# Pooled attention and a mixture of adapters on one core: queries of chunks 4 to 7 turned by DMA, the second batch's sums spread, and the gates' path one period later

## The chip, the cores and the metric

The kernel runs on one core of a Trainium2 chip. Its five engines work in order, each on its own queue of instructions: TensorE (PE, products of matrices and transposes), VectorE (DVE), ScalarE (ACT, here the exponentials), GpSimd (POOL) and SyncE (SP, which issues the transfers). They wait for one another by semaphores. The metric is the time of one execution on the device in microseconds (us); a smaller time is better. The median of three runs before the change is 381.48 us.

## What is computed

```python
def _attn_ref(q, kv, w_sr):                # q (4, 12288, 128), kv (4, 384, 32, 128)
    kv_pool = kv.reshape(B, H // 4, 4, W // 4, 4, C).mean(axis=(2, 4))
    k = v = kv_pool.reshape(B, -1, C) @ w_sr          # 768 keys for each batch
    s = q @ k.transpose(0, 2, 1) / np.sqrt(C)
    a = np.exp(s - s.max(-1, keepdims=True))
    a /= a.sum(-1, keepdims=True) + 1e-09
    return a @ v

def _moe_ref(x, w_gate, A, B):             # x: the 49152 rows of the attention
    logits = x @ w_gate                    # 8 adapters, the best two of each row
    ...
    w = softmax of the two chosen logits
    delta = sum over the two chosen e of w[e] * ((x @ A[e]) @ B[e])    # rank 16
    return x + delta
```

The weights `w_sr`, `w_gate`, `A` and `B` are small; `q`, `kv` and the result are 25 MB each in fp32.

## The kernel before

**Tiles and periods.** The 49152 queries are 96 chunks of 512 (`NCH`), 24 for each of the four batches (`CPB`). The loop of L653 takes c from 2 to 94, and I call one turn of it period c. In period c PE makes three groups of scores for chunks ahead (`scores(x, r)`, r = 0 to 2, each two products L303 for 256 of the 768 keys, followed by an exponential of 128x1024 on ACT, L304), weighs the values of chunk c - 1 in two halves (`weigh`, L315, twelve products each), and does the adapters' work of earlier chunks. `next_scores` takes the next group from the list `todo`. The scores go through two PSUM buffers, `stile`, which the keys' and values' steps use as well, so a group waits until the exponential two groups before has read its buffer.

**After the weighing.** `normalise(c - 1)` on DVE divides by the sum and finds the maxima of the logits (L322, L326, L333); it frees the one PSUM buffer of `weigh`. In even periods `gate(c // 2 - 1)` makes the arguments of a pair's gates on POOL (L342 to L346), and behind it `cast_q` turns the queries of a later pair of chunks into f16 (L107). In odd periods `gate_tanhs((c - 3) // 2)` takes the tanh on ACT (L358), and at the period's end `send_gates` turns the gates on DVE (L402) and stores them in a DRAM tile (L403). `load_gates` fetches them back, spread over the partitions (L410). `gated_hidden(x)` multiplies the hidden values by them on DVE (L420); `up` and `give` make the output rows (L463, L477) and store a pair of chunks (L495). How many periods after its weighing a chunk's hidden values are made is `lag`: 9 for chunks under 57, then 8, 7 and 6. At lag 9 a pair's fetch is issued three periods after its store's, at the start of an even period.

**The queries.** `load_q` reads 1024 queries, `cast_q` makes them f16, `turn_q` transposes them by a DMA (L114) into `qT`; there are two buffers of `q32`, three of `q16`, five of `qT`. The queries of chunks 0 to 7 go another way: `q0` and `q1`, 1 MB each, are transposed in fp32 on PE (`queries`, L567) and copied out by ACT (chunks 0 to 3) or DVE (4 to 7).

**The keys and values.** `load_row` reads a quarter of a kv tile (512 KB); `sum_row` and `sum_cols` add it up, for batch 0 on DVE, for the others on POOL (L173, L177, L178). The steps `pooled_transposed`, `values` and `keys` follow on PE and ACT. `plan(b)` writes down in which period each load (`at`), each add (`sm`) and each step (`st`, then two and three periods later) stands. `squares` and `ranges` gather sums for a check of the values' size.

**What sets the order.** It is written out by hand: each engine does its instructions in program order. SyncE issues nearly all transfers from one queue, in the order: in an odd period query load, output store, kv rows, gates' store; in an even one gates' fetch, turn, kv rows. A wait in it holds up all that follow.

**The start.** Ahead of the loop the three tiles of batch 0 are added up as they land (L593 to L596), `tile_keys` and `tile_values` make keys and values, and the first scores are put between them; `warm` gives PE empty products to do. Before period 2 the groups of chunks 0 and 1 and the groups (2,0), (2,1), (3,0) have been made. At the ends of periods 6 and 8 a fourth group is made (L717).

Of the kernel before, what the change touches and what calls it, by code (L numbers as in the profile page):

```python
# [10 lines left out]
FP32 = mybir.dt.float32  # L11
# [4 lines left out]
AF = mybir.ActivationFunctionType  # L16
# [5 lines left out]
def kernel(  # L22
# [10 lines left out]
    nc = tc.nc  # L33
    P = 128
    B, N, C = q.tensor.shape
# [5 lines left out]
    NTOK = 512  # L41
    NS = NTOK // P
    VW = C + E + 1
    CPB = N // NTOK
    NCH = B * CPB
# [8 lines left out]
    qpool = ctx.enter_context(tc.tile_pool(name="qpool", bufs=3))  # L54
# [17 lines left out]
    mm = nc.tensor.matmul  # L72
# [8 lines left out]
    NT = NJ // 2  # L81
# [16 lines left out]


    def load_q(i):  # L100
        q32[i] = qpool.tile([P, 2, NS * C], FP32, tag="q32", name="q32", bufs=2)
        nc.sync.dma_start(q32[i], qflat[i * HROWS:(i + 1) * HROWS].rearrange(
            "(k p s) c -> p k (s c)", p=P, s=NS))

    def cast_q(i):
        q16[i] = qpool.tile([P, HROWS], F16, tag="q16", name="q16", bufs=3)
        nc.gpsimd.tensor_copy(q16[i], q32[i].rearrange("p k n -> p (k n)"))  # L107

    def new_qT(i):
        qT[i] = qpool.tile([P, 2 * NS, P], F16, tag="qT", name="qT", bufs=5)  # L110
# [1 line left out]
    def turn_q(i):  # L112
        new_qT(i)
        nc.sync.dma_start(qT[i], q16[i], transpose=True)  # L114
# [3 lines left out]
    for t in range(NT):  # L118
        load_kv(0, t)
        if t == 0:  # L120

            nc.sync.dma_start(q0, qflat[0:GROWS].rearrange("(k p s) c -> p k s c", p=P, s=NS))
    nc.sync.dma_start(q1, qflat[GROWS:2 * GROWS].rearrange("(k p s) c -> p k s c", p=P, s=NS))

    w_in = const.tile([P, P], FP32)
    nc.scalar.dma_start(w_in, w_sr)
# [53 lines left out]
    def stile(name):  # L180
        return ps_s.tile([P, 2, NTOK], FP32, tag="sg", name=name)
# [27 lines left out]
    def tile_keys(t, between=lambda: None):  # L209

        k = slice(2 * t * P, 2 * (t + 1) * P)
        kp_ps = ps_t.tile([P, 2 * P], FP32, tag="tp", name="kp_ps")
        for u in range(2):
            mm(kp_ps[:, u * P:(u + 1) * P], kvt[0, t][:, 0, u, 0:C], id_f32, is_transpose=True,
               start=(u == 0), stop=(u == 1), skip_group_check=True)
        if t < NT - 1:
            nc.scalar.activation(kpT[0][:, k], kp_ps, AF.Copy)
        else:
            nc.vector.tensor_copy(kpT[0][:, k], kp_ps)
        between()  # L220
        k_ps = mtile([P, 2 * P], name="k_ps")
        mm(k_ps, w_sr_sb, kpT[0][:, k], start=True, stop=True)
        nc.scalar.activation(kfT[0][:, k], k_ps, AF.Copy)

    def tile_values(t):
        v_ps = mtile([P, 2, C + E], name="v_ps")
# [28 lines left out]
    def plan(b):  # L255
        c0 = CPB * (b - 1)
        if b == 1:
            at = [2, 2, 3, 4, 5, 6, 6, 8, 9, 10, 10, 12]
            sm = [5, 5, 7, 9, 9, 11, 13, 13, 15]
            st = [10, 14, 18]  # L260
        else:
            at = [-11, -9, -7, -5, -5, -3, -1, 1, 1, 3, 5, 7]
            sm = [-3, -1, 1, 3, 5, 7, 9, 11, 13]
            st = [4, 10, 16]
        for i, k in enumerate(at):
            loads.setdefault(c0 + k, []).append((b, i // 4, i % 4))
# [291 lines left out]

    for i in range(4):
        new_qT(i)

    def queries(g, k, t):

        for i in range(NS):
            mm(t[:, i * P:(i + 1) * P], (q0, q1)[g][:, k, i], id_f32, is_transpose=True,  # L567
               start=(i == 0), stop=(i == NS - 1), skip_group_check=True)
        qt = qT[2 * g + k // 2][:, k % 2 * NS:(k % 2 + 1) * NS].rearrange("p s t -> p (s t)")
        if g == 0:  # L570
            nc.scalar.activation(qt, t, AF.Copy)
        else:
            nc.vector.tensor_copy(qt, t)
# [13 lines left out]
    a_bf = const.tile([P, P], BF16)  # L587
    b_half = const.tile([P, P], FP32)
    b_bf = const.tile([P, P], BF16)
    load_q(4)  # L590
    load_q(5)
    cast_q(4)
    for t in range(NT):  # L593
        for d in range(1, 4):
            sum_row(0, t, d, nc.vector)
        sum_cols(0, t, nc.vector)  # L596
        if t == 0:
            nc.vector.tensor_copy(a_bf.rearrange("p (r e) -> p e r", e=E),
                                  a_f.rearrange("p (e r) -> p e r", e=E))
# [3 lines left out]
    tile_keys(0, lambda: queries(0, 0, x_bank()))  # L603
    queries(0, 1, x_bank())
    scores(0, 0)
    tile_values(0)
    queries(0, 2, x_bank())
    scores(1, 0)
    queries(0, 3, x_bank())
    scores(2, 0)  # L610
    scores(3, 0)
    warm(8)
    tile_keys(1)
    warm(2)
    scores(0, 1)
    tile_values(1)
    scores(1, 1)
    weigh(0, 0)
    warm(2)
    tile_keys(2, lambda: queries(1, 0, stile("q_ps")[:, 0]))  # L620
    queries(1, 1, t_bank())
    scores(0, 2)
    tile_values(2)
    scores(2, 1)
    queries(1, 2, t_bank())
    weigh(0, 1)
    scores(1, 2)
    normalise(0)

    todo = [(x, r) for x in range(2, NCH) for r in range(3) if (x, r) not in ((2, 0), (2, 1), (3, 0))]

    def next_scores():
        if todo:
            scores(*todo.pop(0))

    NQ = NCH // GRP

    def lag(c):

        return next(v for m, v in LAGS if c < m)
# [3 lines left out]
    for x in range(OWN):  # L647
        made.setdefault(x + lag(x), []).append(x)
        ups.setdefault(x + lag(x - 3) + 1, []).append(x)
    for p in range(OWN // 2):  # L650
        sent[2 * p + 3] = p
        fetched[2 * p + 3 + {9: 3, 8: 2, 7: 2, 6: 1}[lag(2 * p + 1)]] = p
    for c in range(2, NCH - 1):  # L653
        b, k = divmod(c, CPB)
        if c in fetched and lag(2 * fetched[c] + 1) > 8:
            load_gates(fetched[c])
        if c % 2 == 0 and c // 2 + 3 < 2 * NQ:
            turn_q(c // 2 + 3)
        if c % 2 and (c + 11) // 2 < 2 * NQ:
            load_q((c + 11) // 2)  # L660
        if c == 2:
            load_q(6)
        next_scores()
        if c == 2:
            queries(1, 3, t_bank())
        weigh(c - 1, 0)
        if c == NCH - 2:
            down(c - 4, stile("h_ps")[:, 0])
            apply_gate(c - 4)
        next_scores()  # L670
        if c >= 3 and c % 2 == 1:
            gate_tanhs((c - 3) // 2)
        for x in made.get(c, ())[:-1]:
            gated_hidden(x, t_bank())
        for x in ups.get(c, ()):
            up(x, None if x == ups[c][-1] else t_bank())
            give(x)
        if c in fetched and lag(2 * fetched[c] + 1) <= 8:
            load_gates(fetched[c])
        weigh(c - 1, 1)  # L680
        prep_step(c)
        if c == CUT + 5:
# [36 lines left out]

# [285 lines left out]
```

## Time and profile before

| | us |
|---|---|
| median of three runs | 381.48 |
| lowest, highest | 381.07, 382.75 |
| the profiled execution, whole | 382.61 |
| its span, first to last instruction | 380.8 |
| PE busy | 362.9 |
| ACT busy | 311.1 |
| DVE busy | 301.7 |
| POOL busy | 224.4 |

A row of an order in time gives the start, the time, engine, line, operation, the tiles (out<-in) with their shapes, and how many were merged; in brackets stand the idle time before it and who ended it. "L303" is a line of the kernel. PEld is PE's loading of weights. The windows give the busy time of each engine in a stretch, and the share in which the DMA engines were busy; a share over 1 means that transfers were waiting on one another. A chain of waits is followed back from the last instruction; a row of it gives start, length and what the time went to.

### The profile page before, as it was taken

To read this page: it belongs to the slowest core of one execution; us is meant where nothing else is said; L and a number is where in the kernel's file an instruction comes from. 1 tells how busy PE (TensorE), PEld (TensorE's weight loads), DVE (VectorE), ACT (ScalarE), POOL (GpSimd) and SP (SyncE) were. 2 spreads that over 40 slices of the span, in tenths; PEclk is the share of its full clock that TensorE was granted. 3 is DMA by queue.
4 is the path that set the end of the run, shared out by engine and by line. 5 is a ranking of instruction groups with operands and counts; after the bars stand their busy time and mean duration, and the time that the engine had idled before them with its cause. 6 is when DMAs were issued, how large, how long until landed. Compare 5 with 4: busy or idle time off the path is not lost.

```text
span 380.8 us, 10632 instructions
## 1 busy us (share of the span) xinstructions
PE 362.9 (95%) x3962; PEld 267.7 (70%) x3963; DVE 301.7 (79%) x951; ACT 311.1 (82%) x392; POOL 224.4 (59%) x374
## 2 busy tenths in 40 slices
PE   4989989999999999999999999999999999999993
PEld 1447757677777777777777777777777777767682
DVE  2686556878788888888888888888888898898983
ACT  1547999888888888888888988988888888888853
POOL 1002699996898877764689877755524335232244
PEclk9999999999999999999999999999999999999998
DMA  8996799999999999999999999999899799883325
GB/s 253 364 386 205 203 271 303 300 310 256 365 296 302 309 326 259 312 288 320 320 289 304 338 279 299 278 246 243 175 298 256 196 226 243 182 220 119 136 86 195
DMA packets 93465, 100.47 MB, mean 264 GB/s; under 512 B 56676, under 2 KB 56932, under 8 KB 93412
## 3 DMA queue, kind: packets, MB, share of 16 engines
q1 hardware_dynamic: 91940, 99.58, 96.1%
q8 instruction: 31, 0.51, 0.6%
q10 hardware_dynamic: 1472, 0.20, 0.3%
q14 instruction: 22, 0.18, 0.1%
HBM read 62.33 MB, written 25.90 MB: 232 GB/s over the span
## 4 chain that ended last, share of the span: by engine, by line
PE 73%; DMA 9%; DVE 7%; POOL 7%; issue 2%; ACT 1%; SPq 0%; ACTq 0%; POOLq 0%; DVEq 0%
PE xps L315 30%; PE sg L303 26%; PE d_ps L463 5%; PE t_ps L382 4%; DMA kvt<-in_kv_dram 4%; PE h_ps L417 4%; DMA b_f<-in_moe_B_dram 3%; POOL kvt L173 2%; DVE xn L326 2%; DMA ge<-g_h 2%; DVE ht L420 1%; PE v_ps L197 1%; DVE top L333 1%; POOL q L107 1%; POOL kvt L177 1%
## 5 line engine op out<-in xcount | busy, mean ns | idle before, releaser
L304 ACT ACTIVATE tt<-sg 128x1024 f16<-128x1024 f32 x288 | 277.5, 1022 | 34.8 <-PE sg L303 33.9
L303 PE MATMUL sg<-qT,kfT 128*128 128x512 f16 x576 | 170.1, 379 | 2.4 <-ACT tt L304 1.6
L315 PEld LDWEIGHTS <-tt 128*128 128x128 f16 x2304 | 148.0, 98 | 27.0 <-DVE xn L326 17.2
L315 PE MATMUL xps<-vext,tt 128*128 128x137 f16 x2256 | 166.3, 223 | 0.0
L477 DVE TENSOR_TENSOR osb<-d_ps,xn 128x512 f32<-128x512 f32 x85 | 58.7, 691 | 30.6 <-PE d_ps L463 30.4
L342 POOL TENSOR_TENSOR arg<-xn,top 128x64 f32<-128x64 f32 x47 | 14.8, 315 | 107.3 <-DVE top L333 91.5
L326 DVE TENSOR_TENSOR xn<-xps,rinv_all 128x548 f32<-128x548 f32 x94 | 68.5, 728 | 3.2
L303 PEld LDWEIGHTS <-kfT 128*128 128x128 f16 x576 | 49.3, 98 | 27.1 <-issue 3.9
L173 POOL TENSOR_TENSOR kvt<-kvt 128x1024 f32<-128x1024 f32 x27 | 63.8, 2362 | 0.2
L107 POOL CAST q<-q 128x1024 f16<-128x1024 f32 x44 | 45.7, 1038 | 26.6 <-DMA q<-in_q_dram 26.6
L420 DVE SCALAR_TENSOR_TENSOR ht<-ge,h_ps 128x512 bf16<-128x512 f16 x87 | 58.5, 672 | 0.6 <-DMA ge<-g_h 0.3
L463 PEld LDWEIGHTS <-ht 128*128 128x128 bf16 x368 | 27.2, 97 | 23.6 <-DVE ht L420 3.9
L333 DVE MAX8 top<-xn 128x8 f32<-128x8 f32 x376 | 35.1, 156 | 6.3
L393 DVE COPY xt<-t_ps 128x512 bf16<-128x512 bf16 x92 | 36.7, 399 | 0.0
L382 PE MATMUL t_ps<-id_bf,xn 128*128 128x128 bf16 x376 | 36.3, 219 | 0.0
L463 PE MATMUL d_ps<-b_bf,ht 128*128 128x128 bf16 x340 | 32.9, 219 | 0.3 <-DVE ht L420 0.2
L417 PE MATMUL h_ps<-xt,a_bf 128*128 128x512 bf16 x86 | 32.6, 379 | 0.1
L322 DVE RECIPROCAL rinv_all<-xps 128x4 f32<-128x4 f32 x94 | 17.1, 182 | 15.4 <-PE xps L315 13.1
L382 PEld LDWEIGHTS <-xn 128*128 128x128 bf16 x376 | 26.0, 98 | 0.3
L345 POOL TENSOR_SCALAR msk<-msk 128x64 f32<-128x64 f32 x47 | 20.2, 429 | 4.1
L346 POOL TENSOR_TENSOR arg<-arg,msk 128x64 f32<-128x64 f32 x47 | 15.1, 321 | 3.9
L344 POOL TENSOR_TENSOR arg<-arg,msk 128x64 f32<-128x64 f32 x47 | 15.0, 320 | 3.7
(149 smaller groups left out, 229.4 us busy)
## 6 DMA issues: line engine op xcount, KB each, us to landing
kvt<-in_kv_dram SPq DMA_DIRECT2D x48, 512.0 KB
q<-in_q_dram SPq DMA_DIRECT2D x44, 512.0 KB
out_dram<-osb SPq DMA_DIRECT2D x44, 512.0 KB
ge<-g_h SPq DMA_DIRECT2D x45, 256.0 KB
q<-in_q_dram SPq DMA_DIRECT2D x2, 1024.0 KB
out_dram<-osb SPq DMA_DIRECT2D x8, 256.0 KB
g_h<-g_sb SPq DMA_DIRECT2D x45, 16.0 KB
qT<-q SPq DMA_TRANSPOSE x44
```

The costliest lines, as they stand in the source:

```text
L107: nc.gpsimd.tensor_copy(q16[i], q32[i].rearrange("p k n -> p (k n)"))
L173: eng.tensor_tensor(v[:, 0], v[:, 0], v[:, d], op=ALU.add)
L303: mm(sg[:, k], kfT[b][:, j * P:(j + 1) * P], qc, start=True, stop=True)
L304: nc.scalar.activation(tt[c][:, 2 * r:2 * r + 2], sg, AF.Exp, bias=0.0, scale=scale)
L315: mm(o, tt[c][:, j, s * P:(s + 1) * P], vext[b][:, j, 0:VW], start=(j == 0 and s % 2 == 0), stop=(j == NJ - 1 and s % 2 == 1), skip_group_ ...
L326: nc.vector.tensor_tensor(xn[c].rearrange("p (b s) v -> p b s v", b=2), xv, ri.rearrange("p (b s) -> p b s", b=2).unsqueeze(3).broadcast_t ...
L333: nc.vector.max(gin[c // 2][:, (c % 2) * NS + s], xn[c][:, s, C:C + E])
L382: mm(columns(t_ps, c, s), src[:, s], id_bf, is_transpose=True, start=(s == 0), stop=(s == NS - 1), skip_group_check=True)
L417: mm(h_ps, a_bf, xT[c], start=True, stop=True)
L420: nc.vector.scalar_tensor_tensor(hgT[c].rearrange("p (k a) t -> p k (a t)", k=2), gE[c // 2][:, h:h + NS // 2].rearrange("p a t k -> p k ( ...
L463: mm(dps[c][:, s], columns(hgT[c], c, s), b_bf, start=(s == 0 and fresh), stop=(s == NS - 1), skip_group_check=True)
L477: nc.vector.tensor_tensor(osb[:, lo:hi], d, xn[c][:, lo:hi, 0:C], op=ALU.add)
```

## The change

It has these parts:

- The queries of chunks 4 and 5 and of 6 and 7 (`q32[2]`, `q32[3]`) are loaded in halves into the place of `q1`, with the loads of the next two pairs between; they are cast (`cast_half` on DVE for the first, `cast_q(3)` on POOL for the second) and turned by DMA ahead of the loop. The products of `queries` for them, and their copies on DVE, go. `q32` has three buffers.
- In the start, groups (3,1) and (2,2) are made ahead of the loop, (2,1) earlier than before; the extra groups at the ends of periods 6 and 8 go. The third tile's keys are copied by DVE. Four warming products go.
- For the second batch (`b == 1`) loads, adds and steps stand in other periods.
- At lag 9 the tanh, the turning and the store of a pair's gates stand one period later, in even periods, and so does the fetch, now at the start of odd periods, ahead of the query load.
- The squares of the first two batches stand two periods later.

```diff
     def load_q(i):
-        q32[i] = qpool.tile([P, 2, NS * C], FP32, tag="q32", name="q32", bufs=2)
+        q32[i] = qpool.tile([P, 2, NS * C], FP32, tag="q32", name="q32", bufs=3)
...
-    nc.sync.dma_start(q1, qflat[GROWS:2 * GROWS].rearrange("(k p s) c -> p k s c", p=P, s=NS))
+
+    def load_half(i):
+        q32[i] = q1[:, 2 * i - 4:2 * i - 2].rearrange("p k s c -> p k (s c)")
+        nc.sync.dma_start(q32[i], qflat[i * HROWS:(i + 1) * HROWS].rearrange(
+            "(k p s) c -> p k (s c)", p=P, s=NS))
+
+    load_half(2)
+    load_q(4)
+    load_half(3)
+    load_q(5)
...
-        nc.scalar.activation(kfT[0][:, k], k_ps, AF.Copy)
+        if t < NT - 1:
+            nc.scalar.activation(kfT[0][:, k], k_ps, AF.Copy)
+        else:
+            nc.vector.tensor_copy(kfT[0][:, k], k_ps)
...
         if b == 1:
-            at = [2, 2, 3, 4, 5, 6, 6, 8, 9, 10, 10, 12]
-            sm = [5, 5, 7, 9, 9, 11, 13, 13, 15]
-            st = [10, 14, 18]
+            at = [2, 2, 3, 4, 5, 5, 6, 8, 9, 9, 11, 13]
+            sm = [3, 5, 6, 8, 9, 10, 12, 14, 16]
+            st = [9, 13, 19]
...
-    load_q(4)
-    load_q(5)
+    new_q16(2)
+    cast_q(3)
     cast_q(4)
+
+    def cast_half(k):
+        nc.vector.tensor_copy(q16[2][:, k * NTOK:(k + 1) * NTOK], q32[2][:, k])
...
-    warm(8)
+    warm(6)
     tile_keys(1)
     warm(2)
     scores(0, 1)
     tile_values(1)
     scores(1, 1)
     weigh(0, 0)
-    warm(2)
-    tile_keys(2, lambda: queries(1, 0, stile("q_ps")[:, 0]))
-    queries(1, 1, t_bank())
+
+    def during():
+        cast_half(0)
+        scores(2, 1)
+
+    tile_keys(2, during)
+    cast_half(1)
+    turn_q(2)
+    turn_q(3)
+    scores(3, 1)
     scores(0, 2)
     tile_values(2)
-    scores(2, 1)
-    queries(1, 2, t_bank())
+    scores(1, 2)
     weigh(0, 1)
-    scores(1, 2)
+    next_scores()
     normalise(0)
...
+    tanhs = {}
+    for p in range(NCH // 2 - 2):
+        tanhs[2 * p + 3 + (lag(2 * p + 1) > 8)] = p
     for p in range(OWN // 2):
-        sent[2 * p + 3] = p
-        fetched[2 * p + 3 + {9: 3, 8: 2, 7: 2, 6: 1}[lag(2 * p + 1)]] = p
+        sent[2 * p + 3 + (lag(2 * p + 1) > 8)] = p
+        fetched[2 * p + 3 + {9: 3 + (lag(2 * p + 3) > 8), 8: 2, 7: 2, 6: 1}[lag(2 * p + 1)]] = p
...
-        if c == 2:
-            queries(1, 3, t_bank())
...
-        if c >= 3 and c % 2 == 1:
-            gate_tanhs((c - 3) // 2)
+        if c in tanhs:
+            gate_tanhs(tanhs[c])
...
-        if k in (17, 19, 21) and b + 1 < B:
+        k0 = 19 if b == 0 else 17
+        if k in (k0, k0 + 2, k0 + 4) and b + 1 < B:
             if b == 0:
-                squares(0, (k - 17) // 2)
-            squares(b + 1, (k - 17) // 2)
+                squares(0, (k - k0) // 2)
+            squares(b + 1, (k - k0) // 2)
...
-        if c in (6, 8):
-            next_scores()
```

More of the change, by code (lines that the diff above doesn't have):

```diff
@@ L105, in cast_q, with new_q16 @@
     def cast_q(i):
+        new_q16(i)
+        nc.gpsimd.tensor_copy(q16[i], q32[i].rearrange("p k n -> p (k n)"))
+    def new_q16(i):
         q16[i] = qpool.tile([P, HROWS], F16, tag="q16", name="q16", bufs=3)
-        nc.gpsimd.tensor_copy(q16[i], q32[i].rearrange("p k n -> p (k n)"))
     def new_qT(i):
@@ L557, in all_ok, with queries @@
         nc.vector.tensor_scalar(bad, last, tot, full, op0=ALU.add, op1=ALU.not_equal)
-    for i in range(4):
+    for i in range(2):
         new_qT(i)
-    def queries(g, k, t):
+    def queries(k, t):
         for i in range(NS):
-            mm(t[:, i * P:(i + 1) * P], (q0, q1)[g][:, k, i], id_f32, is_transpose=True,
+            mm(t[:, i * P:(i + 1) * P], q0[:, k, i], id_f32, is_transpose=True,
                start=(i == 0), stop=(i == NS - 1), skip_group_check=True)
[L569 to L573, printed above, removed]
+        qt = qT[k // 2][:, k % 2 * NS:(k % 2 + 1) * NS].rearrange("p s t -> p (s t)")
+        nc.scalar.activation(qt, t, AF.Copy)
     def x_bank():
@@ L602, with next_scores @@
     warm(18)
-    tile_keys(0, lambda: queries(0, 0, x_bank()))
-    queries(0, 1, x_bank())
+    todo = [(x, r) for x in range(2, NCH) for r in range(3) if (x, r) not in ((2, 0), (2, 1), (3, 0), (3, 1))]
+    def next_scores():
+        if todo:
+            scores(*todo.pop(0))
+    tile_keys(0, lambda: queries(0, x_bank()))
+    queries(1, x_bank())
     scores(0, 0)
     tile_values(0)
-    queries(0, 2, x_bank())
+    queries(2, x_bank())
     scores(1, 0)
-    queries(0, 3, x_bank())
+    queries(3, x_bank())
     scores(2, 0)
     scores(3, 0)
-    warm(8)
+    warm(6)
     tile_keys(1)
```

4 lines of the change are left out of this document (removed).

## The prediction

> **What bounds the kernel now.** I read the page first, then the busy time by stretches, then TensorE's instructions in order of time, then what the other engines wait for, and last SyncE's queue.
>
> ```profile
> span 380.8 us, 10632 instructions
> PE 362.9 (95%) x3962; PEld 267.7 (70%) x3963; DVE 301.7 (79%) x951; ACT 311.1 (82%) x392; POOL 224.4 (59%) x374
> 31.00:95.00 64.00, 61.93 (x682) 45.71 (x681) 42.92 (x154) 57.46 (x72) 49.59 (x67) 1.00 1.04 272
> 95.00:260.00 165.00, 165.00 (x1872) 124.97 (x1869) 139.45 (x448) 145.99 (x183) 125.78 (x186) 1.00 1.13 301
> ```
>
> In the last two rows the columns are the stretch, its length, busy time of PE, PEld, DVE, ACT and POOL, the granted clock, the DMA engines' share and GB/s. From 95 to 260 us PE is busy without a gap: what the change does off PE there can only cost. Between 31 and 95 us PE lacks 2 us outright, and its order shows more. The first group of twelve weighted sums (L315) of a period marks it; I call its start the period's start.
>
> ```profile
> 36.26 0.89 PE L315 MATMUL xps<-vext,tt 128*128 128x137 f16 x12
> ...
> 45.51 0.89 PE L315 MATMUL xps<-vext,tt 128*128 128x137 f16 x12
> ...
> 49.32 0.59 PE L303 MATMUL sg<-qT,kfT 128*128 128x512 f16 x2 [0.66 <-ACT tt L304]
> 49.75 0.88 PE L315 MATMUL xps<-vext,tt 128*128 128x137 f16 x12
> ...
> 56.80 0.59 PE L303 MATMUL sg<-qT,kfT 128*128 128x512 f16 x2 [0.72 <-ACT tt L304]
> 57.23 0.88 PE L315 MATMUL xps<-vext,tt 128*128 128x137 f16 x12
> ...
> 60.41 0.88 PE L315 MATMUL xps<-vext,tt 128*128 128x137 f16 x12
> ```
>
> Periods 3, 4 and 5 take 45.51 - 36.26 = 9.25 us, 3.08 each. The next four, 6 to 9, take 14.90 us, where four of 3.08 make 12.33: 2.57 us more. Two of them hold a fourth score group (the extra ones after periods 6 and 8), and PE waits there for the exponentials on ACT. Some 0.10 of it is period 9's first hidden product, so the extra groups cost 2.5 us.
>
> ```profile
> 67.42 0.88 PE L315 MATMUL xps<-vext,tt 128*128 128x137 f16 x12
> ...
> 75.68 0.88 PE L315 MATMUL xps<-vext,tt 128*128 128x137 f16 x12
> ...
> 82.69 0.88 PE L315 MATMUL xps<-vext,tt 128*128 128x137 f16 x12
> ...
> 90.60 0.88 PE L315 MATMUL xps<-vext,tt 128*128 128x137 f16 x12
> ...
> 97.61 0.88 PE L315 MATMUL xps<-vext,tt 128*128 128x137 f16 x12
> ...
> 105.09 0.88 PE L315 MATMUL xps<-vext,tt 128*128 128x137 f16 x12
> ```
>
> ```profile
> 67.29 0.32 ACT L358 ACTIVATE gw_all<-arg 128x64 f16<-128x64 f32 x1 [0.83 <-DVE xn L326]
> ```
>
> ```profile
> 66.94 0.32 POOL L346 TENSOR_TENSOR arg<-arg,msk 128x64 f32<-128x64 f32 x1
> ```
>
> The first six rows are the three pairs of periods (12-13, 16-17, 20-21) in which a tile's values and keys are made: 8.26, 7.91 and 7.48 us for the same work. The third is free of stalls; the first two lose 0.78 + 0.43 = 1.2 us. The two rows after them, of ACT and of POOL, show why: the tanh (L358) starts at 67.29, right after POOL's last gate step ends at 67.26, with 0.83 us of ACT lost before it. The exponentials stand behind it. (The row names DVE, which had long been done.)
>
> **The change, part by part.**
>
> *Scores moved forward.* Two groups, (2,2) and (3,1), move from periods 6 and 8 ahead of the loop, where ACT has room. The loop's periods 6 to 9 become plain: **-2.5**.
>
> *Queries 4 to 7 by DMA.* Sixteen fp32 transposes and three of their four DVE copies leave the stretch before 33 us, the fourth the start of period 2; two DVE casts, one POOL cast and two DMA transposes enter.
>
> ```profile
> 26.79 0.42 DVE L178 TENSOR_TENSOR kvt<-kvt 128x256 f32<-128x256 f32 x1
> ...
> 27.74 0.42 DVE L219 COPY kp_keep<-kp_ps 128x256 f32<-128x256 f32 x1 [0.53 <-PE kp_ps L214]
> ...
> 28.22 0.70 PE L222 MATMUL k_ps<-kp_keep,w_sr_sb 128*128 128x256 f32 x2
> ...
> 30.04 1.94 ACT L304 ACTIVATE tt<-sg 128x1024 f16<-128x1024 f32 x2 [0.70 <-PE sg L303]
> 30.04 1.36 SPq L114 DMA_TRANSPOSE qT<-q  x1
> ...
> 31.17 0.88 PE L315 MATMUL xps<-vext,tt 128*128 128x137 f16 x12
> ```
>
> ```profile
> 31.00:32.00 1.00, 1.00 (x17) 0.97 (x15) 0.63 (x1) 0.97 (x2) 0.00 (x0) 1.00 0.68 136
> 32.00:33.00 1.00, 1.00 (x8) 0.58 (x6) 0.94 (x3) 0.48 (x1) 0.00 (x0) 1.00 0.68 126
> ```
>
> The last kv tile's sums end at 27.21 in both. Afterwards ACT runs the groups (2,1), (3,1), (0,2), (1,2), each 0.97 us (1.94 for two), from about 28.1; (0,2) is then done near 31.3, where it was done near 31.0. So the second half of chunk 0's weighing (31.17) stays where it was or slips 0.2. The PE time saved, four sets of transposes, lies under this ACT chain and is worth nothing by itself. From there two groups less are outstanding, and I put period 3 at 36.2 against 36.26: **0**, bounds -0.4 to +0.5. The copy of the third tile's keys goes from ACT to DVE, which takes it off this chain. Four warming products go; the granted clock is 1.00 in the rows around them, and they fill time in which PE waits for kv: 0.
>
> Group (4,0), the first that needs a DMA-turned query, falls due at about 33.8. Its turn waits for the second DVE cast, behind the copy of the keys: 27.7 + 0.42 for the copy, 0.7 for the keys' product, 0.4 for its copy and 0.4 to 0.7 for the cast (the DVE copies here take 0.42 for 256 elements, and twice the elements cost at most twice) give 29.7 to 30.1. The one turn that stands alone was issued at 30.04 and its 256 KB (136 + 126 GB/s for 1 us each) were through before 33.0: 3 us. So (4,0) is ready at 32.7 to 33.1, **0**, with 0.7 us of cover. The second turn lands some 1.4 us later and is due in period 4, near 39.
>
> The Trainium skill, SBUF — State Buffer, section "SBUF: two separate sides", speaks against this place: a GpSimd instruction and a VectorE copy in a two-port mode hold one port pair exclusively, and the loser waits for the whole instruction. No row of before has such a pair side by side. By it the DVE casts could wait out both POOL casts. It is the third rival's mechanism.
>
> *The second batch's sums spread, and q32 with three buffers.* No work is added: nine row adds and three pairs of column adds keep their cost, but begin in period 3 instead of 5, and the keys' first step comes one period earlier (9, 13, 19 for 10, 14, 18). With the third buffer a query load no longer stands in SyncE's queue for a POOL cast two pairs back, so the kv rows behind it are issued sooner: 0 by itself.
>
> ```profile
> 62.50 0.39 PE L189 MATMUL kp_ps<-id_f,kvt 128*128 128x128 f32 x2
> ```
>
> ```profile
> 65.36 0.31 POOL L342 TENSOR_TENSOR arg<-xn,top 128x64 f32<-128x64 f32 x1
> ...
> 67.20 1.04 POOL L107 CAST q<-q 128x1024 f16<-128x1024 f32 x1
> 68.20 2.36 POOL L173 TENSOR_TENSOR kvt<-kvt 128x1024 f32<-128x1024 f32 x1
> 70.64 1.27 POOL L177 TENSOR_TENSOR kvt<-kvt 128x512 f32<-128x512 f32 x1
> 71.99 0.73 POOL L178 TENSOR_TENSOR kvt<-kvt 128x256 f32<-128x256 f32 x1
> ```
>
> Gate steps, cast, a row and the columns take POOL 72.72 - 65.36 = 7.36 us. For tile 0 that block starts when chunk 5's maxima are there, about 3.4 us after period 6 starts (45.4): 48.9 to 56.2. PE reaches the tile's transposes 1.9 us into period 9 (54.7): 56.6. For tile 1, gate, cast and row of period 8 (5.2), the row of period 9 (2.4) and the block again end at 71.2; PE is there at 68.9 + 2.1 (62.50 - 60.41) = 71.0. So the margin is about nothing at both, and PE, in order, stands if POOL is late: I charge **+0.3**, bounds 0 to +1.2.
>
> *Tanh one period later.* At lag 9 the tanh no longer stands in ACT's queue ahead of a POOL result that is still being made: it has a period of slack, and POOL's backlog above stays under that. **-1.2**. The squares, two periods later (19, 21, 23), now meet the third batch's first adds twice:
>
> ```profile
> L241 POOL TENSOR_TENSOR sq<-vext 128x272 f32<-128x272 f16 x12 | 7.7, 642 | 0.2
> ...
> L245 POOL TENSOR_TENSOR sq<-sq,sq 128x272 f32<-128x272 f32 x8 | 6.1, 761 | 0.6
> ```
>
> two of each are 2.8 us, so such a pair of periods gives POOL 1.84 + 1.04 + 2.36 + 2.8 = 8.0 us in some 7.0; over two pairs it falls 2 us behind, inside the slack: 0.
>
> *Turning, store and load later.* Their number is the same; the fetch has one period less before its use, and moves in SyncE's queue behind a turn and in front of a query load.
>
> ```profile
> 50.45 9.03 DMA kvt<-in_kv_dram
> ...
> 324.72 6.45 DMA ge<-g_h
> ```
>
> ```profile
> 122.11 0.57 SPq L410 DMA_DIRECT2D ge<-g_h  x1
> ```
>
> ```profile
> 130.77 0.69 DVE L477 TENSOR_TENSOR osb<-d_ps,xn 128x512 f32<-128x512 f32 x1 [0.62 <-PE d_ps L463]
> ...
> 132.83 0.67 DVE L420 SCALAR_TENSOR_TENSOR ht<-ge,h_ps 128x512 bf16<-128x512 f16 x1
> ```
>
> The first two rows are links of the chain that ended last: a gate fetch took 6.45 us from issue to use, a kv row 9.03. The eleventh fetch is issued at 122.11 and first used at 132.83: 10.7 us. One period (7.48 / 2 = 3.7) less leaves 7.0. At 6.45 it is there in time; at 9.03 it is 2.0 us late, of which DVE's gap before the next output add hides 0.62. The DMA share of 1.13 in this stretch says that the queue is always full, so the truth lies between; the row of the same kind (6.45) is the nearer one. **+0.4**, bounds 0 to 1.4 for each pair of chunks that is late.
>
> *Sum:* -2.5 + 0 + 0.3 - 1.2 + 0.4 = **-3.0 us**. The profiled execution took 382.61 us (span 380.8, 1.8 around it), 1.1 above the median; its own forecast is 379.6, and on the median of 381.48 it is **378.5**.
>
> **Rivals.**
>
> *The fetch is late in the two stretches with kv loads* (the third and fourth batch's rows), and each time the shift settles after one stall of 2.0 - 0.62 = 1.4 us: -3.0 - 0.4 + 2.8 = -0.6, **380.9**. For it speaks the full queue; against it, that it was never late before 260 us.
>
> *The fetch is late at every pair while kv rows load (slower).* Store and fetch are themselves timed by PE, so waiting buys no lead. Beyond 7.0 + 0.62 = 7.6 us from issue to landing every such pair pays; the loads run through about 20 pairs. A mean excess of 0.3 us costs 6 us: **384.5**. It turns the change into a loss once the mean excess passes 0.17, that is at a mean of 7.8 us, inside the 6.45 to 9.03 seen. Against it: a slower PE asks less of the queue.
>
> *The start slips.* The DVE casts wait for POOL's two (1.04 each), (4,0) comes 0.8 us late, and PE stands at both tiles of the second batch for 0.5 more each: -3.0 + 1.8 = -1.2, **380.3**.
>
> *The extra score groups were free* (ACT is the limit anyway and the groups must run somewhere): then only the 1.2 us stay and the charges eat 0.7: **381.0**. Against it: ACT has its gap before 30.04.
>
> **Chances.** Forecast 0.52, fetch late twice 0.15, late at every pair 0.18, start slips 0.10, groups free 0.05. The forecast's own range is 377.2 to 379.9. A change of 0.5% (1.9 us, to 379.6 or 383.4) is about what a measurement of this kernel tells from none. Faster by that: nearly all of the forecast's 0.52 and a part of the start's and the twice-late case, 0.57. Slower: most of the every-pair case and a little for what I have not seen, 0.19. Within: 0.24. The range reaches from all gains without charges (-3.7, and the -0.4 of the start's bound, with a little below) to where the every-pair case has cost its first 5 us: 376.8 to 383.4.
>
> **What would show it.** After: periods 6 to 9 at 3.1 us each with no PE wait for ACT of 0.6 or more; no ACT idle before tanh of 0.4; no PE wait for the sums (L177/L178) at the second batch's transposes; (4,0) not waiting for the turn; the DVE product L420 not waiting for the fetch. If DVE waits at L420 between 95 and 260 us, or PE is busy less than the whole of that stretch, the last part was mis-priced and the time lies above 380.

## The result and the profile after

The changed kernel takes **378.6 us** (median of seven runs, 377.93 to 379.46) against 381.48 before (seven runs beside it, 381.07 to 382.75): a ratio of 0.9926, 95% interval 0.9909 to 0.9943. The forecast was 378.5. The same kernel measured again, beside other runs of before (median 381.43), gave 379.11 and 0.9934 (0.991 to 0.9957), so the gain is 2.3 to 2.9 us.

First the page of the changed kernel, then its busy time in the two stretches of before, with the same columns (stretch, length, PE, PEld, DVE, ACT, POOL, clock, DMA share, GB/s).

```profile
span 376.8 us, 10584 instructions
PE 359.5 (95%) x3943; PEld 265.0 (70%) x3943; DVE 300.4 (80%) x950; ACT 310.1 (82%) x391; POOL 225.1 (60%) x375
```

```profile
31.00:95.00 64.00, 63.32 (x713) 47.10 (x713) 44.52 (x161) 58.07 (x72) 51.57 (x71) 1.00 1.10 297
95.00:260.00 165.00, 164.23 (x1859) 124.25 (x1857) 139.37 (x453) 144.78 (x183) 123.42 (x182) 1.00 1.11 301
```

From 31 to 95 us PE now lacks 0.68 us where it lacked 2.07. From 95 to 260, where it lacked nothing, it lacks 0.77: a stall that the change made. PE's order of time shows the places (lines have moved by 12 to 15: weighing is L330, a pooled tile's transposes L201, the third adds of its columns L190).

```profile
43.52 0.89 PE L330 MATMUL xps<-vext,tt 128*128 128x137 f16 x12
...
46.60 0.89 PE L330 MATMUL xps<-vext,tt 128*128 128x137 f16 x12
...
49.69 0.89 PE L330 MATMUL xps<-vext,tt 128*128 128x137 f16 x12
...
52.77 0.89 PE L330 MATMUL xps<-vext,tt 128*128 128x137 f16 x12
...
54.98 0.44 PE L201 MATMUL kp_ps<-id_f,kvt 128*128 128x128 f32 x2 [0.17 <-POOL kvt L190]
...
56.56 0.88 PE L330 MATMUL xps<-vext,tt 128*128 128x137 f16 x12
...
70.03 0.44 PE L201 MATMUL kp_ps<-id_f,kvt 128*128 128x128 f32 x2 [0.34 <-POOL kvt L190]
...
127.12 0.38 PE L432 MATMUL h_ps<-xt,a_bf 128*128 128x512 bf16 x1
...
129.85 0.40 PE L478 MATMUL d_ps<-b_bf,ht 128*128 128x128 bf16 x4 [0.77 <-DVE ht L435]
```

Periods 6, 7 and 8 are plain: 3.08, 3.09 and 3.08 us. Period 9, in which the first tile's transposes begin, takes 3.79 (52.77 to 56.56). In it, and in period 13, PE stands 0.17 and 0.34 us for POOL's column sums. The last row is the new stall: PE waits 0.77 us in period 30 for a gated hidden product (`ht`).

To compare executions I use one number for each period: when the first weights of its weighing are loaded, counted from those of chunk 0 (period 1). Weights are loaded a little ahead of the products, so a period measured this way can differ from the rows above (period 9: 3.58). The number leaves out when an execution's first weighing starts, which varies between executions of one kernel: 25.74 us in the profiled execution of before and 24.42 in another of it, 23.88 and 24.09 in two of the changed kernel, and up to 26.81 in the kernels below that have its start unaltered. So 1.86 of the 4.0 us between the two spans (380.8 and 376.8) are put down to this spread. Against the second execution of before, in us (minus is earlier):

| | start of period 3 | 10 | 27 | 31 | 95 | median | ratio, 95% interval |
|---|---|---|---|---|---|---|---|
| before, first profile | +0.03 | +0.05 | +0.12 | +0.12 | +0.08 | 381.48 | |
| changed, first profile | -0.10 | -2.04 | -2.85 | -1.91 | -2.23 | 378.6 | 0.9909 to 0.9943 |
| changed, again | -0.02 | -2.11 | -3.26 | -2.25 | -2.57 | 379.11 | 0.991 to 0.9957 |
| tanh part undone | +0.15 | -0.16 | +0.65 | +1.17 | +0.84 | 382.69 | 1.0021 to 1.006 |
| groups back in the loop | -0.31 | -0.05 | -1.41 | -0.56 | -0.89 | 380.15 | 0.9957 to 0.9997 |
| before, tanh part alone | +0.04 | +0.02 | -1.22 | -1.20 | -0.71 | 381.04 | 0.9961 to 1.0016 |
| before, groups alone | +1.86 | +0.69 | +2.04 | +2.04 | +2.24 | 383.7 | 1.0029 to 1.0075 |
| queries on PE again | +0.73 | -1.34 | -2.68 | -2.68 | -1.93 | 379.51 | 0.9911 to 0.9957 |
| steps later | -0.10 | -2.52 | -3.77 | -2.45 | -2.76 | 378.96 | 0.9918 to 0.9973 |
| second batch's plan of before | -0.09 | -2.51 | -3.75 | -3.08 | -3.39 | 379.01 | 0.9912 to 0.9956 |
| turn in odd periods | -0.64 | -1.49 | -2.29 | -2.28 | -2.59 | 379.13 | 0.9904 to 0.9949 |
| the last two together | -0.10 | -2.53 | -3.70 | -3.56 | -3.53 | 379.21 | 0.9914 to 0.9955 |
| turn in odd, steps later | -0.09 | -2.50 | -3.42 | -2.30 | -2.62 | 379.47 | 0.9918 to 0.9987 |

Each ratio is against runs of before made beside it (their medians are 381.43 to 381.56). Two executions of before agree within 0.15 us all the way, two of the changed kernel within 0.45; so I read differences of 0.5 us and more in these columns. That rests on two pairs, and the start can shift one execution by as much: with the turn in odd periods period 3 stands at -0.64, though nothing differs ahead of it. In the changed kernel 2.1 us are gained up to period 10, another 0.8 to 1.15 up to period 27, and 0.94 to 1.01 are lost in period 30.

The waits of ACT ahead of the gates' tanh tell the rest. The view of one line of the kernel names, over the whole execution, who ended its idle time (us, times). Of the kernel before:

```profile
L358 ACT ACTIVATE gw_all<-arg x45: 307/314/331, 38.6 to 350.8; 128x64 f16<-128x64 f32 x45
...
its engine sat idle before it (us, times) until:
  POOL arg L346: 2.8, 7
  DVE xn L326: 0.8, 1
```

Of the changed kernel the same view has no row under that heading: 45 tanhs, none with a wait.

```profile
L373 ACT ACTIVATE gw_all<-arg x45: 307/309/333, 39.7 to 346.6; 128x64 f16<-128x64 f32 x45
...
its engine sat idle before it (us, times) until:
who waited for it (us, times):
```

Last the stall of period 30: SyncE's issues and the hidden product, in order of time, of the changed kernel.

```profile
117.27 4.35 SPq L117 DMA_TRANSPOSE qT<-q  x1
121.72 0.60 SPq L418 DMA_DIRECT2D g_h<-g_sb  x1
122.36 0.59 SPq L425 DMA_DIRECT2D ge<-g_h  x1
```

```profile
129.10 0.69 DVE L435 SCALAR_TENSOR_TENSOR ht<-ge,h_ps 128x512 bf16<-128x512 f16 x1 [1.02 <-PE sg L318]
```

The eleventh pair's fetch is issued at 122.36. By the trace's records of the transfers its last part lands at 129.01, 6.65 us later, and DVE's product, after 1.02 us of idle time, starts 0.09 behind. The bracket names PE's scores, but the product doesn't read them: the hidden values that it reads were done at 127.50 (127.12 + 0.38, in PE's order above). So the wait is for the fetch. In the second profile of this kernel the same product starts again 0.09 us after the landing, and further down are kernels in which the same wait names the fetch outright.

### The profile page after: what moved, and what is told of

Same layout as the page of the kernel before. It is cut to its first block, busy times and chain, and to the rows that moved or that the text cites. A ratio compares the mean times of both kernels' runs of the same rounds, so it can differ in the third digit from the quotient of the medians.

```text
span 376.8 us, 10584 instructions
## 1 busy us (share of the span) xinstructions
PE 359.5 (95%) x3943; PEld 265.0 (70%) x3943; DVE 300.4 (80%) x950; ACT 310.1 (82%) x391; POOL 225.1 (60%) x375
## 4 chain that ended last, share of the span: by engine, by line
PE 78%; DVE 7%; POOL 7%; DMA 4%; issue 1%; ACT 1%; ACTq 0%; SPq 0%; POOLq 0%; DVEq 0%
PE xps L330 32%; PE sg L318 28%; PE d_ps L478 5%; PE t_ps L397 5%; PE h_ps L432 4%; DMA b_f<-in_moe_B_dram 3%; POOL kvt L185 2%; DMA kvt<-in_kv_dram 2%; DVE xn L341 2%; DVE ht L435 1%; PE v_ps L209 1%; DVE kvt L185 1%; POOL q L107 1%; POOL kvt L189 1%; PE kp_ps L201 1%
## 5 line engine op out<-in xcount | busy, mean ns | idle before, releaser
L330 PEld LDWEIGHTS <-tt 128*128 128x128 f16 x2304 | 147.7, 98 | 28.5 <-DVE xn L341 18.6
L330 PE MATMUL xps<-vext,tt 128*128 128x137 f16 x2256 | 166.5, 223 | 0.3 <-DVE xn L341 0.2
L107 POOL CAST q<-q 128x1024 f16<-128x1024 f32 x45 | 46.8, 1041 | 24.8 <-DMA q<-in_q_dram 24.6
```

The source lines that it names most:

```text
L330: mm(o, tt[c][:, j, s * P:(s + 1) * P], vext[b][:, j, 0:VW], start=(j == 0 and s % 2 == 0), stop=(j == NJ - 1 and s % 2 == 1), skip_group_ ...
```

## The experiments

**The two kernels again.**

> The kernel before once more, for a second look at its start. In the two profiles, before and after, chunk 0's first weighing starts 1.86 us apart (25.74 and 23.88 us), although no instruction differs ahead of it but transfers that are issued later. Theory: this is the spread between executions of the start, and this profile's start lies anywhere from 23.8 to 26 us, while from there to the last chunk's weighing it repeats the first profile within 0.3 us (342 us). Rival: the change speeds the start, then this start lies again at 25.5 to 26.

> The changed kernel once more. Theory: 2.5 to 3.3 us faster than the kernel before in the timed rounds; in the profile, from chunk 0's first weighing to chunk 95's, 2.1 us shorter than before, with the wait of DVE for the eleventh gate fetch in period 30 again (0.5 to 1.2 us). Rival (the start is faster by the change): the same ratio, but a start at 23.6 to 24.2 us in every profile.

Measured: 381.21 in the one run of before, within 0.15 us of the first profile at each period of the table; 379.11 for the changed kernel, with the stall of period 30 again (4.82 us where 3.80 is the rule). By medians that is 2.3 us faster, a little less than the 2.5 expected; in the profile the stretch up to chunk 95's weighing is 2.3 to 2.4 shorter, in place of 2.1. The rivals, by which the change speeds the start, fall: before started at 24.42 here, and kernels with the changed start as late as 26.81. In these two pairs, what differs most between executions of one kernel is the start.

**The tanh part, undone in the changed kernel and alone in the old one.**

```diff
-        tanhs[2 * p + 3 + (lag(2 * p + 1) > 8)] = p
+        tanhs[2 * p + 3] = p
...
-        sent[2 * p + 3 + (lag(2 * p + 1) > 8)] = p
-        fetched[2 * p + 3 + {9: 3 + (lag(2 * p + 3) > 8), 8: 2, 7: 2, 6: 1}[lag(2 * p + 1)]] = p
+        sent[2 * p + 3] = p
+        fetched[2 * p + 3 + {9: 3, 8: 2, 7: 2, 6: 1}[lag(2 * p + 1)]] = p
```

> The changed kernel with the gates' tanh, turning, store and fetch at lag 9 back where they were. Theory: the stall of period 30 (0.94 us) is gone, and ACT's waits for POOL ahead of the tanh in the second batch's periods are back and cost 0.7 to 1.4 us, so the time is within 0.6 us of the changed kernel, 378.5 to 379.5. Rival (the later fetch is late at many pairs): 1.5 us or more faster than the changed kernel. Rival (the tanh costs nothing): 0.9 us faster.

> The kernel before with the last part of the change alone: at lag 9 the pair's tanh, turning, store and fetch one period later. The second batch's sums and squares, the queries and the groups as before. Theory of the prediction: the waits of weighed sums for the tanh in the second batch go, -1.2 us, and late fetches give back up to 0.9: 380.2 to 381.2. Rival from the reversed experiment (undoing this part in the changed kernel cost 3.6 us): the part is worth about that by itself, 377.9 to 378.6, and then it carries the whole change.

Undone, 382.69: 3.6 us slower than the changed kernel and slower than before. The theory had the cost much too small, and both rivals expected a faster kernel. PE's waits in this kernel, and ACT's ahead of the tanh:

```profile
45.45 0.59 PE L318 MATMUL sg<-qT,kfT 128*128 128x512 f16 x2 [0.69 <-ACT tt L319]
...
58.11 0.59 PE L318 MATMUL sg<-qT,kfT 128*128 128x512 f16 x2 [0.98 <-ACT kp_keep L203]
...
118.28 0.59 PE L318 MATMUL sg<-qT,kfT 128*128 128x512 f16 x2 [1.21 <-ACT tt L319]
```

```profile
44.17 0.32 ACT L373 ACTIVATE gw_all<-arg 128x64 f16<-128x64 f32 x1 [0.88 <-POOL arg L361]
...
57.47 0.32 ACT L373 ACTIVATE gw_all<-arg 128x64 f16<-128x64 f32 x1 [0.99 <-POOL arg L361]
...
117.00 0.32 ACT L373 ACTIVATE gw_all<-arg 128x64 f16<-128x64 f32 x1 [1.77 <-POOL arg L361]
```

```profile
L373 ACT ACTIVATE gw_all<-arg x45: 307/312/332, 37.0 to 349.8; 128x64 f16<-128x64 f32 x45
...
  POOL arg L361: 6.8, 9
```

The pairs of rows are cause and effect: ACT stands 0.88, 0.99 and 1.77 us for the gates' arguments, and about a microsecond later PE stands 0.69, 0.98 and 1.21 for what is queued behind the tanh on ACT. Over the execution ACT loses 6.8 us in nine such waits, where before had 3.6 in eight.

Not all of it belongs to the score groups. 3.25 of the 6.8 us lie in three waits between 108 and 125 us (in before 0.86 in two), long after the groups, and periods 26 and 28 are 1.36 and 0.53 us longer than before. POOL's order there:

```profile
109.75 2.37 POOL L185 TENSOR_TENSOR kvt<-kvt 128x1024 f32<-128x1024 f32 x1
112.07 0.65 POOL L256 TENSOR_TENSOR sq<-vext 128x272 f32<-128x272 f16 x1
...
115.08 0.31 POOL L357 TENSOR_TENSOR arg<-xn,top 128x64 f32<-128x64 f32 x1
...
116.65 0.32 POOL L361 TENSOR_TENSOR arg<-arg,msk 128x64 f32<-128x64 f32 x1
```

The squares (L256 and L260), put two periods later by the change, follow a row of the third batch's sums in two pairs of periods, at 104 and at 112 us, where in before they did so in one; POOL works without a wait from 98.8 to 122.4 us, and its last gate step ends at 116.97, 0.03 before the tanh. So in the changed kernel the late tanh covers this other part of the change as well.

Alone in the old kernel the part does what the prediction charged: the start of period 27 comes 1.22 us earlier (forecast -1.2), the waits ahead of the tanh are gone, and a late fetch costs 0.44 in period 54 (4.24 for 3.80). The time, 381.04, is inside the theory's range and can't be told from before. The rival, by which this part carries the whole change, falls.

**The score groups, back in the changed kernel and ahead in the old one.** First the groups (3,1) and (2,2) leave the start and the fourth groups of periods 6 and 8 come back; then the old kernel with the opposite edit, its queries all on PE (the two groups also leave `todo`):

```diff
+    scores(3, 1)
     scores(0, 2)
...
     scores(1, 2)
+    scores(2, 2)
     normalise(0)
...
-        if c in (6, 8):
-            next_scores()
```

> The changed kernel with groups (2,2) and (3,1) back in the loop and the extra groups at the ends of periods 6 and 8. Theory: periods 6 to 9 are longer by 2.3 us again and the time is 380.6 to 381.2, so most of the gain is gone. Rival (the groups were free, ACT being the limit in any case): the time stays within 0.5 us of the changed kernel.

> The kernel before with one thing of the change alone: score groups (3,1) and (2,2) issued before the loop, and no further groups in periods 6 and 8; all queries on TensorE. Theory: periods 6 to 9 fall to about 3.1 us each and the loop ends 2.0 to 2.3 us earlier, 379.2 to 379.6. Rival (the moved groups cost the same where they go, and the earlier start of the second batch meets POOL's sums): half of it is given back by period 14, 380.3 to 380.9.

Back in the loop: 380.15, 1.0 slower, between the two theories; at period 10 all of the early gain is gone (-0.05), at the end 1.7 of it is still missing. Ahead in the old kernel: 383.7, **slower** than before by 0.29% to 0.75%, past what either theory allowed. Its table row splits this. Period 3 starts 1.86 us late, which is what two exponentials of 0.97 us each take on ACT: without the rest of the change the start has no room for them. And period 6 falls to 3.08, as expected, but periods 8 and 10 take 4.34 and 4.58 where before had 4.17 and 3.51. The same views as above, of this kernel:

```profile
54.74 0.59 PE L303 MATMUL sg<-qT,kfT 128*128 128x512 f16 x2 [1.10 <-ACT tt L304]
...
62.07 0.59 PE L303 MATMUL sg<-qT,kfT 128*128 128x512 f16 x2 [0.91 <-ACT tt L304]
```

```profile
53.47 0.32 ACT L358 ACTIVATE gw_all<-arg 128x64 f16<-128x64 f32 x1 [1.29 <-POOL arg L346]
...
60.79 0.32 ACT L358 ACTIVATE gw_all<-arg 128x64 f16<-128x64 f32 x1 [1.18 <-POOL arg L346]
```

```profile
L358 ACT ACTIVATE gw_all<-arg x45: 307/314/331, 39.7 to 352.2; 128x64 f16<-128x64 f32 x45
...
  POOL arg L346: 6.1, 9
```

Taking the extra exponentials off ACT lets it come to the tanh sooner, and it stands there: 6.1 us of idle time in place of 3.6. The extra groups had filled that hole.

The start of period 95 of the four kernels and of the changed one, against before: tanh part alone -0.71, groups alone +2.24, the changed kernel without the tanh part +0.84, without the groups -0.89, whole -2.57. In the changed kernel the groups are worth 1.7 and the tanh part 3.4 (of which the stall of period 30, absent without it, already takes off 1.0); neither alone in the old one gives a gain that the time shows. The changed kernel's other parts, the queries, the plan and the squares, are in only some of the five, so this is no clean test of the groups and the tanh by themselves.

**The queries.** Chunks 4 to 7 transposed on PE again, one set each in the place of a DVE cast or behind a step, `q1` loaded whole and not cast, the groups kept ahead of the loop:

```diff
     def during():
-        cast_half(0)
+        queries(0, stile("q_ps")[:, 0], 1)
         scores(2, 1)
...
-    cast_half(1)
-    turn_q(2)
-    turn_q(3)
+    queries(1, t_bank(), 1)
     scores(3, 1)
     scores(0, 2)
     tile_values(2)
+    queries(2, t_bank(), 1)
     scores(1, 2)
...
+        if c == 2:
+            queries(3, t_bank(), 1)
```

> The changed kernel with the queries of chunks 4 to 7 transposed by PE and copied by DVE again, the moved score groups kept ahead of the loop. Theory (what decides there is ACT's chain of exponentials, the four sets of transposes lie under it): counted from chunk 0's first weighing, period 3 starts 0 to 0.4 us later than in the changed kernel, and the time is within 0.5 us of it. Rival (PE decides there): period 3 starts 1.3 to 1.8 us later and the time is 1.3 us or more above the changed kernel.

Period 3 starts 0.75 us later than in the changed kernel, between the two theories, and period 10 still 0.77. The end is 0.64 later. The time doesn't show it: the median is 0.4 higher (379.51), the ratio to before the same (0.9934). So in the trace PE's time in the start wasn't free. The stall of period 30 is gone here, and one of the same size stands in period 54 (4.85 us for 3.80): a late fetch again, by the idle time that the view of DVE's hidden product lists.

```profile
its engine sat idle before it (us, times) until:
  PE t_ps L431: 1.5, 3
  DMA ge<-g_h: 1.1, 1
```

**The second batch's plan.** Only the steps one period later or more, or all of before's plan (and its squares):

```diff
-            st = [9, 13, 19]
+            st = [10, 14, 19]
```

```diff
-            at = [2, 2, 3, 4, 5, 5, 6, 8, 9, 9, 11, 13]
-            sm = [3, 5, 6, 8, 9, 10, 12, 14, 16]
-            st = [9, 13, 19]
+            at = [2, 2, 3, 4, 5, 6, 6, 8, 9, 10, 10, 12]
+            sm = [5, 5, 7, 9, 9, 11, 13, 13, 15]
+            st = [10, 14, 18]
...
-        k0 = 19 if b == 0 else 17
+        k0 = 17
```

> The changed kernel with the first two key steps of the second batch one period later (10, 14, 19 for 9, 13, 19). Theory: PE's waits for POOL's column sums at these transposes (0.17 and 0.34 us in the first profile of the changed kernel) are gone, 0.2 to 0.6 us less by period 18. Rival (POOL's lateness shows elsewhere, in the tanh or in the third step): no difference by period 22.

> The changed kernel with loads, sums, steps and squares of the second batch in the periods of before. Theory (the spread sums only move POOL's work forward, the tanh's slack does the rest): within 0.5 us of the changed kernel. Rival (the spread is what keeps the gate arguments in time): 1 us or more above it.

Both bring the waits for column sums in periods 9 and 13 to nothing and start period 27 at -3.77 and -3.75, 0.5 earlier than the changed kernel. The spread sums, then, gain nothing in these traces once the tanh is late; with their earlier steps they cost those 0.5. The medians (378.96, 379.01) don't show it: period 30 takes 5.12 and 4.47 in these two profiles.

**The turn behind the fetch.** The stall of period 30 comes after a turn that holds SyncE for 4.35 us ahead of the gates' store and fetch. Here the turn moves into odd periods, behind the fetch; then the same with the plan of before, and with the later steps.

```diff
-        if c % 2 == 0 and c // 2 + 3 < 2 * NQ:
-            turn_q(c // 2 + 3)
+        if c == 2:
+            turn_q(4)
+        if c % 2 and c >= 5 and (c - 1) // 2 + 3 < 2 * NQ:
+            turn_q((c - 1) // 2 + 3)
```

> The changed kernel with the DMA turn of the queries issued one period later, in odd periods behind the gates' fetch, so that no turn stands between a store's data and its issue. Theory (the turn holds SyncE for 4.3 us in this stretch and so delays store and fetch of the pair behind it): the stall of period 30 is gone, 0.9 us less than the changed kernel, 377.7 to 378.4. Rival (the fetch is late because the DMA engines are full, whoever is issued first): the stall stays within 0.3 us of 0.94.

> The changed kernel with two edits together: the second batch's sums, weighing steps and squares by the plan of before, and turn_q issued behind the fetch in odd periods. Alone the first moved the end of the loop by -0.8 us in the trace and the second removed the stall of period 30 (-1.0) but had a wait of 1.2 us in period 9 for the spread column sums. Theory: with the old plan the wait of period 9 is gone as well, and the two gains add: the loop ends 1.5 to 2.0 us earlier than in the changed kernel, counted from chunk 0's first weighing, period 30 at 3.8 us, a median of 377 to 378. Rival: the stall only moves to another pair (as it moved to period 54 with the queries on TensorE), and the gain is the 0.8 of the old plan or less: 378 to 378.6.

> The changed kernel with turn_q in odd periods behind the fetch and the second batch's last column-sum steps one or more periods later (10, 14, 19 in place of 9, 13, 19). Theory: the wait of 1.2 us in period 9 under the turn in odd periods came from the spread sums, so the later steps remove it, and the loop ends 1.0 to 1.6 us earlier than in the changed kernel: 377.3 to 378.2. Rival: the wait of period 9 belongs to the turn (its transfers beside the chunk's loads), stays, and the gain is under 0.5.

Medians 379.13, 379.21 and 379.47, all above the 377 to 378.4 expected: none is faster than the changed kernel. The traces say more. In the first, period 30 is at its 3.80, but PE stands in period 9:

```profile
58.46 0.44 PE L201 MATMUL kp_ps<-id_f,kvt 128*128 128x128 f32 x2 [1.24 <-POOL kvt L190]
```

That wait is absent in the other two, so it needs the early steps. But with them and the turn where it was, it is only 0.17 us. The other 1.07 us are about what two shifts of this execution make: counted from the first weighing, PE is 0.54 us earlier at period 3 than in the changed kernel, and POOL's first row of the batch starts 0.58 later. Whether the moved turn or the late start (26.81) makes this row late isn't shown. With before's plan period 30 takes 3.94 and period 95 starts 0.96 us earlier than in the changed kernel, less than the 1.5 to 2.0 expected, though the largest gain of any trace here. With the later steps the stall is back, 4.92. Its rows, in order of time:

```profile
120.38 0.57 SPq L425 DMA_DIRECT2D ge<-g_h  x1
121.06 3.36 SPq L117 DMA_TRANSPOSE qT<-q  x1
```

```profile
128.83 0.69 DVE L435 SCALAR_TENSOR_TENSOR ht<-ge,h_ps 128x512 bf16<-128x512 f16 x1 [0.68 <-DMA ge<-g_h]
```

```profile
129.66 0.60 PE L318 MATMUL sg<-qT,kfT 128*128 128x512 f16 x2 [0.95 <-DMA qT<-q]
```

Counted from the first weighing (24.51 here, 23.88 in the changed kernel) the fetch is issued 2.6 us earlier than there, but used only 0.9 earlier, 8.45 us after its issue. The turn behind it is late too, and PE waits 0.95 us for its queries. So the order on SyncE is not the whole cause: a fetch issued sooner takes longer. That the backlog of all transfers sets the landing would fit both traces; a run with fewer bytes in this stretch, which would show it, wasn't made. Another reading fits too: a turn issued right behind the fetch holds it up. With a turn behind it the eleventh fetch lands 6.9 to 8.7 us after its issue in six traces of seven (5.7 in the one with the tanh part undone), with a query load behind it 5.7 to 6.9 in all seven. No run separates the two.

## Why the prediction came out right, step by step

- **Scores moved forward (-2.5).** In the changed kernel periods 6 to 8 became plain, and 1.9 to 2.1 us were gained from period 6 to 10; the first tile's transposes, now in period 9, take the rest. As a term of its own it was wrong: the same move in the old kernel costs 2.2 us. The prediction held that ACT has room ahead of the loop and that the loop's periods then "become plain". Neither is so by itself: in the old kernel the start pays the two exponentials in full (1.86 us), and in the loop ACT's time goes into waits for POOL. The gain rests on the room that the new start makes and on the late tanh.
- **Queries by DMA (0).** Period 3 started 0.02 to 0.10 us earlier, inside the bounds. But the reason, that PE's saved time lies under ACT's chain and is worth nothing, fell: put back, it costs 0.75 us there. The 0 is a balance: +1.86 for the groups in the old start, less 0.75 for the transposes and 1.1 for the rest (the third tile's keys copied on DVE, the new order); only the 0.75 was tried alone.
- **Sums spread (+0.3).** PE's waits were 0.17 and 0.34 in the first profile, where the margin had been worked out as about nothing. Taking them away moves period 27 by 0.5, so +0.5 was the price, inside the bounds (0.9 by the first profile).
- **Tanh later (-1.2).** Exact for the old kernel (-1.22). In the changed one the part is worth 3.4 to 3.6. Up to period 10 this is 1.95 us, since the groups ahead bring ACT to the tanh earlier: that is where the missing worth of the first term lies. Periods 26 and 28 give another 1.9, where POOL is late by the squares and the third batch's rows; the stall of period 30 takes 1.0 back. The two terms are not to be priced one by one; their sum, -3.7, is close to what they do together (period 27: -2.85 to -3.26, with the 0.5 for the sums).
- **Turning, store and fetch later (+0.4).** One pair was late, the eleventh, the one that was looked at; it cost 0.94 to 1.01. The fetch took 6.65 us, near the row of 6.45 that the charge went by. That was luck in part: that row is of a fetch at 324.72 us, when no kv rows are loaded any more, while the eleventh fetch of before, by the same trace's records of the transfers, landed 8.55 us after its issue; with that, the reckoning would have had it 1.55 us late. What was mis-sized is the time it had: 7.0 reckoned, but the product would have run 1.02 earlier, at 128.08, 5.7 us after the issue, since the turn ahead of it had held SyncE for 4.35 (the gates to be stored were turned by 118.31, their store was issued at 121.72). No second stall followed. The rival in which every pair is late was near all the same: the thirteenth and fourteenth fetches had a microsecond and 0.3 us to spare. It failed as the fetches landed sooner from their new place: the eighth to the twenty-seventh took 6.9 and 7.4 us in the mean in the two traces of before, 5.8 and 5.9 in the two of the changed kernel.
- **Squares later (0).** Right under the condition that the prediction named, the tanh's slack: with the tanh undone, POOL's backlog of squares and rows stands ahead of the losses of periods 26 and 28. Put back together with the old plan, under the late tanh, they showed no cost. Not tried alone.
- **Start slips.** Both halves of pair 2's queries are cast in time. The rival's mechanism is in the trace, though. The view of the query tiles between 25 and 31 us (times in ns: least, median, most):

```profile
L607 DVE CAST q<-q x2: 417/634/851, 26.2 to 27.4; 128x512 f16<-128x512 f32 x2
L107 POOL CAST q<-q x2: 1037/1134/1232, 26.9 to 27.9; 128x1024 f16<-128x1024 f32 x2
L117 SPq DMA_TRANSPOSE qT<-q x2: 1268/1320/1371, 28.3 to 29.8; - x2
```

The first DVE cast, alone, takes 417 ns; the second, begun at 27.4 beside POOL's, takes 851. The Trainium skill, SBUF — State Buffer, section "SBUF: two separate sides", has one engine wait out the other's instruction on the shared ports. The trace agrees: the DVE cast ends at 28.26, 0.28 us after the first POOL cast (27.98), so it waited out what was left of that one. In the run with the turn in odd periods the first DVE cast ran beside it, took 1147 ns, and ended again 0.28 us after it (29.71 and 29.43). The loss is 0.43 us here and 0.73 there, of one POOL cast and not of both, and here it lay under the chain.

Of the sum of -3.0 the traces have -2.23 and -2.57 at the start of period 95, and the medians -2.9 and -2.3. The forecast of the time was right. But two of its terms hold only together, the squares' zero rests on one of them, and the fetch's charge came from a row of another stretch: that the sum came so near is in part luck.

## What to carry to other kernels

A wait that a profile shows is not the only one that it holds: work that fills an engine can cover a wait right behind it, and moving that work away uncovers it. So price two edits on the same in-order engine together, and when a part is judged, undo it in the new kernel as well as trying it alone in the old: the two answers here were 3.6 us and 0.5 (the 0.5 can't be told from none). A transfer whose slack is cut to its landing time then stalls at a place that changes from edit to edit, and here reordering the issues gave no better time.

## What the runs showed that was not expected

- When the first weighing starts varies from one execution to the next: 23.9 to 25.7 us in most profiles, 26.81 in one. That is as large as the whole gain and hides differences of half a microsecond in the medians.
- The issue of a DMA transpose holds SyncE very unequally: 1.27 and 1.37 us for two at 28 to 30 us (the last row above), 4.35 at 117 us. What stands behind it on SyncE is issued later by as much.
- The old plan, with or without the turn moved, starts period 95 0.8 to 1.0 us earlier in the trace, and gave no better median over twelve runs. Whether its gain is eaten by later starts or by other stalls in the executions that weren't profiled is open.
